# Linear attention and a routed expert layer: twelve expert tiles computed inside attention, fp32 loads on the sync queue, routing per batch

## The chip, the cores and the metric

The kernel runs on one core of one Trainium2 chip. The metric is device time in microseconds (us), the median of several executions. A profiled execution has its own span, which may differ by some us from the median. The engines are named as the profile names them: PE (matmul), PEld (weight load of PE), DVE (VectorE), ACT (ScalarE), POOL (GpSimd), SP (SyncE). The profile counts the core's 16 DMA engines together, whichever engine issues a transfer. PSUM is the memory that the matmuls write, split into tiles here named `..._ps`; a tile pool with two buffers lets one tile be filled while the other is read.

## The reference, cut to what matters

```python
def _attn_ref(q, k, v):                       # q, k, v: (8, 8, 576, 64) fp32
    q_p, k_p = phi(q), phi(k)                 # phi(x) = elu(x) + 1
    kv = np.einsum('bhsd,bhse->bhde', k_p, v)
    z = np.sum(k_p, axis=2)
    num = np.einsum('bhsd,bhde->bhse', q_p, kv)
    den = np.einsum('bhsd,bhd->bhs', q_p, z)[..., None] + 1e-06
    return num / den
# x = attention output as (4608, 512); 8 experts, F = 1024
    noisy_logits = x @ w_gate + np.log1p(np.exp(x @ w_noise)) * noise
    top2 = np.argpartition(-noisy_logits, 2, axis=1)[:, :2]   # and their softmax
    for e in range(E):
        for k in range(2):
            mask = top2[:, k] == e
            h = np.maximum(x[mask] @ w1[e], 0.0)
            out[mask] += top2_w[mask, k, None] * (h @ w2[e])
```

Each token goes to two experts: 9216 rows in all. The kernel sorts them by expert into a DRAM buffer `x_sorted` and gives every expert room for ten tiles of 128 rows, so 80 tiles. A token's second expert must add to what its first one wrote.

## The kernel before: the parts that matter

Stage 1 takes the eight batches in four groups of two: loads (cast to bf16 by GpSimd's DMA), attention, routing, then 18 scatters of 128 rows into `x_sorted`. "Ranking" is the small matmul within routing that gives each row its place. It ends a group's arithmetic, so its start time is a good mark of progress.

```python
        self.ps_kv = pool("A_ps_kv", 2, space=PSUM)     # attention: every PSUM tile twice
        self.ps_t = pool("A_ps_t", 2, space=PSUM)
        self.ps_num = pool("A_ps_num", 2, space=PSUM)
    ...
    for e in range(E):                                   # zero rows behind each expert's region
        r0 = e * REGION + 8 * P
        nc.sync.dma_start(out=x_sorted[r0 : r0 + 2 * P, :].rearrange(...), in_=...)
    with ExitStack() as actx:
        pa = PhaseA(actx, tc, q, k, v, x_sorted, c)
        pa.run()                                         # all attention, then
        for e in range(3):
            pb.load_w(e)                                 # experts
```

Stage 2 takes the experts in turn. Of each expert, transposed loads bring the rows (`xt`), PE makes `h_ps` and `y_ps`, VectorE scales `y`, and GpSimd scatters `y` into the output. From the second expert on, GpSimd first gathers what stands there (`L`), and a gather may not start before all scatters ahead of it have landed.

```python
        for e in range(E):
            ...
            for n in (512, 512, 256):
                ...                                      # load xt, h = relu(x @ w1)
                if prev is not None:
                    flush(prev)                          # y = h @ w2 of the chunk before, scatter
                if t0 == 0:
                    if e + 3 < E:
                        self.load_w(e + 3)
                    for t in range(T_CAP):               # all ten gathers of the expert in one go
                        L[t] = self.gather(gi[:, t : t + 1]) if e > 0 else None
```

## Time and profile before

The kernel before takes 584 us (median of 4 runs, 581 to 589). The profiled execution has a span of 595.4 us; its run took 597.2 us, 2.8% above the fastest. By the measure used for the other runs (slow when over 1.5% above the fastest of the same kernel) it is a slow one, so stage times of the kernel before are in sum some 13 us too long. Where these 13 us lie, no run shows.

The table of windows of the kernel before. Each row is a stretch of the span: from:to, length, then busy us of each engine with its count of instructions, the granted TensorE clock (1.00 is full), the busy share of the DMA engines, GB/s.

```profile
core 0: us, PE busy (x) PEld busy (x) DVE busy (x) ACT busy (x) POOL busy (x), PEclk, DMA share, GB/s
0.00:133.00 133.00, 44.66 (x308) 28.88 (x308) 74.86 (x242) 49.42 (x47) 69.49 (x92) 0.68 1.21 176
133.00:219.00 86.00, 36.01 (x262) 23.79 (x260) 43.23 (x149) 21.34 (x26) 36.05 (x36) 0.52 0.29 80
219.00:251.00 32.00, 0.00 (x0) 0.00 (x0) 6.68 (x38) 0.00 (x0) 17.32 (x18) 0.50 0.34 99
251.00:595.00 344.00, 292.81 (x1408) 141.84 (x1408) 97.04 (x212) 99.41 (x192) 165.84 (x170) 0.92 0.68 143
```

No engine is full before 219 us (VectorE 118 us, PE 81). Then nothing runs on PE for 32 us while the last scatters land and the first rows are loaded. Then PE is busy 293 of 344 us. The rankings, one for each group of two batches, start at 71.9, 127.4, 171.3 and 218.3 us; here they are in the view of one source line (its numbers are durations in ns, then first and last start in us):

```profile
L335 PE MATMUL kv_ps<-A,ut x4: 219/219/219, 71.9 to 218.3; 128*128 128x72 bf16 x4
```

Two groups of the page of the kernel before follow. After the bar stand busy us, mean ns of one, and the idle time of that engine just ahead of them with what ended most of it.

```profile
L483 PE MATMUL y_ps<-w,hT 128*128 128x512 bf16 x640 | 149.8, 392 | 36.5 <-DVE y L489 36.5
...
L461 POOL DMA_INDIRECT L<-out_dram,gi x70 | 70.6, 1009 | 82.1 <-DMA out_dram<-y,si 60.6
```

The gathers' idle time that is ended by a scatter landing, 60.6 us, came in 6 waits (view of waits): about one for each expert. The timeline of GpSimd shows one of them (start, us, instruction, and in brackets the idle time ahead of it):

```profile
445.05 1.08 POOL L461 DMA_INDIRECT L<-out_dram,gi  x1 [14.52 <-DMA out_dram<-y,si]
446.43 1.01 POOL L461 DMA_INDIRECT L<-out_dram,gi  x1 [0.31 <-issue]
...
456.88 1.00 POOL L461 DMA_INDIRECT L<-out_dram,gi  x1 [0.30 <-issue]
460.06 1.02 POOL L490 DMA_INDIRECT out_dram<-y,si  x1 [2.18 <-DVE gi L454]
461.38 0.99 POOL L490 DMA_INDIRECT out_dram<-y,si  x1 [0.30 <-issue]
```

### The profile page before, as it was taken

To read this page: it belongs to the slowest core of one execution; us is meant where nothing else is said; L and a number is where in the kernel's file an instruction comes from. 1 tells how busy PE (TensorE), PEld (TensorE's weight loads), DVE (VectorE), ACT (ScalarE), POOL (GpSimd) and SP (SyncE) were. 2 spreads that over 40 slices of the span, in tenths; PEclk is the share of its full clock that TensorE was granted. 3 is DMA by queue.
4 is the path that set the end of the run, shared out by engine and by line. 5 is a ranking of instruction groups with operands and counts; after the bars stand their busy time and mean duration, and the time that the engine had idled before them with its cause. 6 is when DMAs were issued, how large, how long until landed. Compare 5 with 4: busy or idle time off the path is not lost. (4 is left out here: it accounts for less than half of the span.)

```text
span 595.4 us, 5833 instructions
## 1 busy us (share of the span) xinstructions
PE 373.5 (63%) x1976; PEld 194.5 (33%) x1976; DVE 221.8 (37%) x638; ACT 170.2 (29%) x265; POOL 288.7 (48%) x315
## 2 busy tenths in 40 slices
PE   0173173137245300199989928969948968989984
PEld 0151142015124100045444404425424434444442
DVE  4359655375650560413233104314304304333122
ACT  0466444025021120062333401421511321423410
POOL 6445378427427117204346516725706726565364
PEclk9996555556555555589999978998987998998998
DMA  9999954995602002555864993993893995573153
GB/s 168 210 191 191 191 131 101 192 209 157 124 27 102 36 10 106 128 91 130 184 101 121 184 110 80 228 140 101 217 120 101 243 146 145 189 157 145 57 160 128
DMA packets 122985, 82.65 MB, mean 139 GB/s; under 512 B 74164, under 2 KB 108980, under 8 KB 122944
## 3 DMA queue, kind: packets, MB, share of 16 engines
q0 software_dynamic: 65888, 69.02, 56.8%
q1 hardware_dynamic: 54272, 12.98, 14.8%
q10 hardware_dynamic: 2784, 0.18, 0.4%
q8 instruction: 17, 0.28, 0.2%
q14 instruction: 24, 0.20, 0.1%
HBM read 80.72 MB, written 32.87 MB: 191 GB/s over the span
## 5 line engine op out<-in xcount | busy, mean ns | idle before, releaser
L474 PE MATMUL h_ps<-xt,w 128*128 128x512 bf16 (+1 forms) x768 | 150.5, 355 | 39.5 <-DMA xt<-x_sorted 32.3
L476 ACT ACTIVATE hT<-h_ps 128x512 bf16<-128x512 f32 (+1 forms) x192 | 99.4, 527 | 260.8 <-PE h_ps L474 209.2
L483 PE MATMUL y_ps<-w,hT 128*128 128x512 bf16 x640 | 149.8, 392 | 36.5 <-DVE y L489 36.5
L490 POOL DMA_INDIRECT out_dram<-y,si x80 | 79.4, 992 | 97.4 <-DVE y L487 39.9
L474 PEld LDWEIGHTS <-w 128*128 128x128 bf16 x768 | 77.8, 101 | 111.1 <-issue 46.9
L376 POOL DMA_INDIRECT x_sorted<-xrow,posi x72 | 73.6, 1022 | 78.9 <-DVE xrow L373 33.7
L461 POOL DMA_INDIRECT L<-out_dram,gi x70 | 70.6, 1009 | 82.1 <-DMA out_dram<-y,si 60.6
L483 PEld LDWEIGHTS <-hT 128*128 128x128 bf16 x640 | 64.1, 100 | 115.5 <-issue 45.3
L489 DVE SCALAR_TENSOR_TENSOR y<-y_ps,gate,L 128x512 f32<-128x512 f32 x70 | 51.1, 731 | 98.8 <-PE y_ps L483 60.6
L460 DVE MEMSET L<- 128x512 f32 x70 | 34.0, 485 | 34.4 <-DMA x_sorted<-xrow,posi 24.4
L270 PE MATMUL num_ps<-kvbd,pqt 128*128 128x162 bf16 x128 | 22.2, 324 | 38.6 <-DVE lwt L293 34.6
L203 PE MATMUL kv_ps<-v,phk 128*128 128x192 bf16 x128 | 26.0, 360 | 19.0 <-DVE phk L190 19.0
L335 PE MATMUL kv_ps<-A,ut 128*128 128x72 bf16 x4 | 0.9, 219 | 44.2 <-DVE A L331 44.2
L270 PEld LDWEIGHTS <-pqt 128*128 128x128 bf16 x128 | 13.2, 130 | 45.6 <-DVE lwt L293 41.3
L248 ACT COPY pqt<-t_ps 128x1024 bf16<-128x1024 bf16 x16 | 16.0, 1014 | 32.5 <-PE t_ps L244 10.6
L287 DVE TENSOR_TENSOR xrow<-num_ps,rden 128x512 bf16<-128x512 f32 x36 | 24.7, 687 | 0.5
L444 DVE SCALAR_TENSOR_TENSOR isf<-meta 128x10 f32<-128x10 f32 x8 | 1.4, 174 | 58.5 <-DMA meta<-x_sorted 58.5
L203 PEld LDWEIGHTS <-phk 128*128 128x128 bf16 x128 | 14.1, 131 | 23.6 <-DVE phk L190 19.0
L244 PE MATMUL t_ps<-ident,phq 128*128 128x128 bf16 x128 | 16.0, 306 | 8.0 <-ACT pqt L248 4.5
L185 ACT ACTIVATE e<-kt 128x2048 bf16<-128x2048 bf16 x8 | 15.2, 1912 | 10.7 <-DMA kt<-in_k_dram 7.9
L487 DVE TENSOR_SCALAR y<-y_ps,gate 128x512 f32<-128x512 f32 x10 | 7.5, 750 | 28.7 <-PE y_ps L483 28.7
L244 PEld LDWEIGHTS <-phq 128*128 128x128 bf16 x128 | 13.7, 144 | 9.2 <-issue 9.2
(116 smaller groups left out, 277.2 us busy)
## 6 DMA issues: line engine op xcount, KB each, us to landing
w<-in_moe_w_dram POOLq DMA_DIRECT2D x32, 512.0 KB
kt<-in_k_dram POOLq DMA_DIRECT2D x8, 512.0 KB
v<-in_v_dram POOLq DMA_DIRECT2D x8, 512.0 KB
qt<-in_q_dram POOLq DMA_DIRECT2D x8, 512.0 KB
x_sorted<-zrow SPq DMA_DIRECT2D x8, 264.0 KB, 6.6
out_dram<-y,si POOLq DMA_INDIRECT x80
x_sorted<-xrow,posi POOLq DMA_INDIRECT x72
L<-out_dram,gi POOLq DMA_INDIRECT x70
```

Source lines behind the costliest of these rows:

```text
L203: nc.tensor.matmul(out=ps[:, i, 0:192], lhsT=phk[:, hp, ci, :], rhs=vt[:, hp::4, 64 * ci : 64 * ci + 64], start=(i == 0 and ci == 0), stop ...
L244: nc.tensor.transpose(tp[:, i * 512 + ci * P : i * 512 + ci * P + P], phq[:, 2 * half + i, ci, :], c["ident"][:],)
L270: nc.tensor.matmul(out=ps[:, hp, 0:KVW], lhsT=pqs[j][:, hp, cc * P : cc * P + P], rhs=kvbds[j][:, hp, :], start=(hp % 2 == 0), stop=(hp % ...
L287: nc.vector.tensor_tensor(out=_ap(xrow[:, ci, 0:HD], [[64, 4], [256, 2], [1, 64]]), in0=_ap(ps, [[256, 4], [64, 2], [1, 64]]), in1=_ap(rd, ...
L376: r = nc.gpsimd.indirect_dma_start(out=self.x_sorted, out_offset=bass.IndirectOffsetOnAxis(ap=posi[:, ci, sl : sl + 1], axis=0), in_=xrow[ ...
L460: nc.vector.memset(L[:], 0.0)
L461: nc.gpsimd.indirect_dma_start(out=L[:].bitcast(INT32), out_offset=None, in_=self.out.bitcast(INT32), in_offset=bass.IndirectOffsetOnAxis( ...
L474: nc.tensor.matmul(out=ps[:, 0:n], lhsT=w1[:, dc, fc * P : fc * P + P], rhs=xt[:, dc, 0:n], start=(dc == 0), stop=(dc == 3))
L476: nc.scalar.activation(out=hT[:, fc, 0:n], in_=ps[:, 0:n], func=ACT.Relu)
L483: nc.tensor.matmul(out=ps[:], lhsT=hT[:, fc, t * P : t * P + P], rhs=w2[:, fc, :], start=(fc == 0), stop=(fc == 7))
L489: nc.vector.scalar_tensor_tensor(out=y[:], in0=ps[:], scalar=gate, in1=L[:], op0=ALU.mult, op1=ALU.add)
L490: r = nc.gpsimd.indirect_dma_start(out=self.out, out_offset=bass.IndirectOffsetOnAxis(ap=si, axis=0), in_=y[:], in_offset=None, bounds_che ...
```

## The change

The intent: PE has room during attention, so after four of the eight batches, with half of the tokens routed, the first 512 rows of experts 0, 1 and 2 (12 of the 80 tiles) are computed between the remaining batches. "Round two" then does the other 68 tiles. To feed this, routing is done per batch and not per pair; loads come as fp32 on the sync queue, and VectorE and ScalarE read fp32; ScalarE's queue takes the zero rows. Core of the diff:

```diff
+Q1 = 512
+E1 = 3
...
     for e in range(E):
-        r0 = e * REGION + 8 * P
-        nc.sync.dma_start(
-            out=x_sorted[r0 : r0 + 2 * P, :].rearrange("(t p) c -> p t c", p=P),
-            in_=_ap(zrow, [[0, 2], [1, ROW_W // 2]]),
-        )
+        for r0 in ([8 * P, 9 * P] if e >= E1 else [3 * P, 8 * P, 9 * P]):
+            nc.scalar.dma_start(out=x_sorted[e * REGION + r0 : e * REGION + r0 + P, :], in_=zrow[:])
...
+        ps = self.ps[b % 2] if b < NU // 2 else self.ps[0]     # two PSUM sets, then one
...
-        self.lp = pool("B_l", 12)
-        self.yp = pool("B_y", 6)
+        self.lp = pool("B_l", 4)
+        self.yp = pool("B_y", 3)
...
+        for b in range(NU // 2):
+            pa.batch(b)
+            ...
+        ld2.__exit__(None, None, None)                         # 10 of 16 load buffers
+        ps_extra.__exit__(None, None, None)                    # the second PSUM set
+        pb.open(ctx)
+        pb.psum.append(... "ps_b1", bufs=2 ...)                # ... now serve the experts
+        for b in range(NU // 2, NU):
+            ...
+            e = b - NU // 2
+            if e < E1:
+                pb.expert(e, 0, Q1 // P, col(cnt1, e), e == 0, group="read1")
+            pa.batch(b)
...
+    for e in range(3, 6):
+        pb.load_w(e, 1)
+    for e in range(E):
+        row0 = Q1 if e < E1 else 0
+        pb.expert(e, row0, T_CAP - row0 // P, col(carry, e), False)
+        if e + 6 < E:
+            pb.load_w(e + 6)
...
             hT = self.mm1(w1, xt, n)
             self.flush()
             if not first:
+                for t in range(t0, t0 + n // P):               # gathers of this chunk only: four
+                    L[t] = self.gather(gi[:, t : t + 1])
```

## The prediction

> **What bounds the kernel now.** Three stretches. (1) Attention and routing, 0 to 219 us, the last ranking matmul (timeline): no engine is full; VectorE is busy 116 of 217 us, PE 80 at a granted clock of 0.62 (table of windows). (2) A drain to 251 us: 18 scatters, 1.27 us each, then the transposed loads; PE idles 32.3 us (waits). (3) Experts, to 595 us: 80 row tiles, PE busy 293 of 345 us. At full clock a tile costs 16 matmuls of 216 ns, 3.45 us, 276 us in all; the rest is stalls, mostly GpSimd's gather waiting for the previous scatter to land (60.6 us in 6 waits), worst where a weight load shares the queue (10 to 16 us, against 2.3 without).
>
> **What the change does.**
> - 12 of 80 tiles (41 us of PE at full clock) move into the second half of attention; the last drain has 10 scatters.
> - Loads leave GpSimd's queue, with 16 fp32 buffers: attention should not starve. The nine table loads (1.28 us each) become one.
> - VectorE gets more work: eight routings instead of four (about 10 us each), casts of v, fp32 inputs. "VectorE: DVE Perf Modes" ("The perf-mode tier table") gives fp32 single-source operations 2x where bf16 gets 4x; this trace shows only bf16 (0.69 us for 2048), so I estimate 0.69 us for 1024 fp32. From traced durations I estimate 23 us per batch, 184 for eight, plus 19 for round one (8 memsets of 0.49, 12 outputs of 0.75, small ones): attention becomes VectorE-bound.
> - In the compiled order PE runs experts 0 and 1 of round one inside batch 5; they wait for batch 3's scatters (13 us) and the xt load. VectorE loses about 20 us there.
> - Round two: gathers come four at a time; each group waits until the scatters before it have landed, and the scatters for the gathers. From traced times 4 x 1.3 + 2.4 + 4 x 1.3 + 2.3 = 15.1 us per four tiles, where PE needs 13.8; about 41 us per ten-tile expert against PE's 34.5. GpSimd's chain sets the pace.
> - Weights of experts 3 to 5 (12.6 MB fp32, about 31 us at the traced rate) are issued between the last scatter and the first gather: PE stalls 10 to 20 us.
>
> **Sum (profiled scale).** Last ranking 219 -> 240 us (more VectorE work, fewer waits). From there to the end 376 -> 335 us (slow start and three six-tile experts under weight loads 127, five experts at 41, tail). 595 -> 575; unprofiled runs lie some 10 us lower: 566 us against 585.
>
> **What would show it.** VectorE busy above 80% before the last ranking, near 205 us in total there; last ranking at 225 to 260 us; PE idle 10 us or more before round one's first expert matmul; drain about 20 us; each group of gathers idle 2 to 3 us before it; ten-tile experts 38 to 43 us apart.
>
> **What would make it wrong.** Faster: routing hides in VectorE's gaps and ranking ends near 215 us, or PE's four output buffers hide GpSimd's chain. Slower: fp32 casts hold up descriptor writing ("SBUF — State Buffer", "Who interferes with whom": two-port VectorE operations block GpSimd; this trace shows scatters stretching from 0.96 to 1.48 us beside VectorE work), or round one stalls longer.
>
> Prediction 566 us, 8 in 10 between 530 and 603; faster 0.57, same 0.26, slower 0.17.

## The result and the profile after

The changed kernel takes 664.6 us (median of 4 runs, 664.2 to 667.1) against 584.4 us: slower, ratio 1.138 [1.129, 1.146]. A ratio here is the mean time of one kernel's fast runs over that of the other's of the same rounds, so it is not quite the ratio of the medians. The profiled span is 662.7 us.

The rankings of the changed kernel are now eight; these are their lines in PE's timeline:

```profile
60.51 0.19 PE L371 MATMUL kv_ps<-A,ut 128*128 128x32 bf16 x1
...
81.16 0.19 PE L371 MATMUL kv_ps<-A,ut 128*128 128x40 bf16 x1 [6.80 <-DVE A L367]
...
108.73 0.18 PE L371 MATMUL kv_ps<-A,ut 128*128 128x32 bf16 x1 [9.83 <-DVE A L367]
...
135.41 0.19 PE L371 MATMUL kv_ps<-A,ut 128*128 128x40 bf16 x1 [0.89 <-DVE A L367]
...
159.70 0.19 PE L371 MATMUL kv_ps<-A,ut 128*128 128x32 bf16 x1 [18.23 <-DVE A L367]
...
225.74 0.19 PE L371 MATMUL kv_ps<-A,ut 128*128 128x40 bf16 x1 [6.46 <-DVE A L367]
...
263.47 0.18 PE L371 MATMUL kv_ps<-A,ut 128*128 128x32 bf16 x1 [3.28 <-DVE A L367]
...
289.30 0.19 PE L371 MATMUL kv_ps<-A,ut 128*128 128x40 bf16 x1 [6.46 <-DVE A L367]
```

The first four batches are ranked at 135.4 us (before: 127.4). The other four need 154 us (before: 91). The table of windows of the changed kernel, cut at these marks:

```profile
core 0: us, PE busy (x) PEld busy (x) DVE busy (x) ACT busy (x) POOL busy (x), PEclk, DMA share, GB/s
0.00:135.00 135.00, 46.10 (x332) 29.69 (x333) 87.06 (x355) 44.52 (x60) 32.74 (x43) 1.00 0.98 251
135.00:160.00 25.00, 2.03 (x19) 1.34 (x18) 17.76 (x83) 5.71 (x10) 12.29 (x12) 1.00 0.80 232
160.00:226.00 66.00, 38.86 (x202) 18.12 (x206) 34.63 (x122) 19.98 (x31) 22.63 (x20) 0.91 0.53 135
226.00:289.00 63.00, 30.14 (x186) 16.94 (x186) 28.40 (x126) 12.55 (x22) 22.78 (x23) 0.61 0.21 65
289.00:314.00 25.00, 6.49 (x21) 2.51 (x22) 8.32 (x44) 0.00 (x0) 17.97 (x20) 0.57 0.50 135
314.00:437.00 123.00, 94.53 (x425) 44.67 (x432) 27.10 (x85) 32.98 (x64) 38.90 (x40) 0.85 0.84 153
437.00:648.00 211.00, 164.67 (x773) 79.14 (x784) 59.54 (x113) 53.54 (x104) 100.35 (x101) 0.92 0.41 117
```

VectorE is busy 168 us of the first 289, 58%, and in the second half of attention 81 of 154. It is not the bound. PE is not either (71 of 154). From 314 to 437 us the three shortened experts of round two run (18 tiles in 123 us), from 437 to 648 the five of ten tiles, 42 us each, where ten tiles at full PE speed take 34.5.

The same groups of the page, after:

```profile
L535 PE MATMUL y_ps<-w,hT 128*128 128x512 bf16 x628 | 162.9, 414 | 54.2 <-DVE y L541 49.6
...
L513 POOL DMA_INDIRECT L<-out_dram,gi x76 | 77.5, 1020 | 91.7 <-DMA out_dram<-y,si 61.2
```

The gathers now wait 61.2 us in 21 waits (view of waits) instead of 60.6 in 6, and PE waits more for VectorE's reads of `y_ps` (49.6 us, before 36.5). One period of GpSimd's timeline in a ten-tile expert:

```profile
482.67 1.04 POOL L513 DMA_INDIRECT L<-out_dram,gi  x1 [3.64 <-DMA out_dram<-y,si]
484.02 1.02 POOL L513 DMA_INDIRECT L<-out_dram,gi  x1 [0.31 <-issue]
...
486.64 1.00 POOL L513 DMA_INDIRECT L<-out_dram,gi  x1 [0.30 <-issue]
490.72 1.02 POOL L542 DMA_INDIRECT out_dram<-y,si  x1 [3.08 <-DVE L L512]
...
494.63 0.97 POOL L542 DMA_INDIRECT out_dram<-y,si  x1 [0.30 <-DVE y L541]
498.18 1.04 POOL L513 DMA_INDIRECT L<-out_dram,gi  x1 [2.58 <-DMA out_dram<-y,si]
```

Four gathers, a wait until they have landed, four scatters, a wait until they have landed: 482.67 to 498.18 is 15.5 us for four tiles.

### The profile page after: what moved, and what is told of

It reads as the page before. It is cut to its first block, busy times and chain, and to the rows that moved or that the text cites. A ratio compares the mean times of both kernels' runs of the same rounds, so it can differ in the third digit from the quotient of the medians.

```text
span 662.7 us, 6183 instructions
## 1 busy us (share of the span) xinstructions
PE 382.8 (58%) x1953; PEld 192.4 (29%) x1980; DVE 262.8 (40%) x922; ACT 169.3 (26%) x289; POOL 248.6 (38%) x257
## 5 line engine op out<-in xcount | busy, mean ns | idle before, releaser
L535 PE MATMUL y_ps<-w,hT 128*128 128x512 bf16 x628 | 162.9, 414 | 54.2 <-DVE y L541 49.6
L423 POOL DMA_INDIRECT x_sorted<-xrow,posi x72 | 75.9, 1054 | 163.0 <-DMA ld<-in_q_dram 61.9
L541 DVE SCALAR_TENSOR_TENSOR y<-y_ps,gate,L 128x512 f32<-128x512 f32 x76 | 55.2, 729 | 164.1 <-DMA L<-out_dram,gi 86.6
L513 POOL DMA_INDIRECT L<-out_dram,gi x76 | 77.5, 1020 | 91.7 <-DMA out_dram<-y,si 61.2
L535 PEld LDWEIGHTS <-hT 128*128 128x128 bf16 x640 | 66.3, 104 | 142.6 <-issue 77.8
L195 ACT ACTIVATE e<-ld 128x1024 bf16<-128x1024 f32 x32 | 33.6, 1054 | 54.4 <-DVE phk L199 12.7
L303 PE MATMUL num_ps<-kvbd,pqt 128*128 128x162 bf16 x128 | 23.2, 320 | 39.9 <-DVE lwt L326 34.5
L512 DVE MEMSET L<- 128x512 f32 x76 | 36.9, 485 | 10.4 <-DVE y L541 6.9
L243 PE MATMUL kv_ps<-v,phk 128*128 128x130 bf16 x128 | 19.2, 303 | 37.0 <-DVE phk L199 25.7
L243 PEld LDWEIGHTS <-phk 128*128 128x128 bf16 x128 | 11.9, 130 | 40.7 <-DVE phk L199 25.7
L196 DVE TENSOR_SCALAR t<-ld 128x1024 bf16<-128x1024 f32 x32 | 21.7, 685 | 2.4 <-DMA ld<-in_k_dram 2.2
```

What stands on the lines that cost most here:

```text
L195: nc.scalar.activation(out=e[:], in_=flat, func=ACT.Exp)
L243: nc.tensor.matmul(out=ps[:, i, 0:130], lhsT=phk[:, i, ci, :], rhs=vt[:, hp, ci, :], start=(i == 0 and ci == 0), stop=False, skip_group_ch ...
L303: nc.tensor.matmul(out=ps[:, hp, 0:KVW], lhsT=pqt[:, hp, ci * P : ci * P + P], rhs=kvbds[-1][:, hp, :], start=(hp % 2 == 0), stop=(hp % 2 ...
L423: r = nc.gpsimd.indirect_dma_start(out=self.x_sorted, out_offset=bass.IndirectOffsetOnAxis(ap=posi[:, ci, sl : sl + 1], axis=0), in_=xrow[ ...
L512: nc.vector.memset(L[:], 0.0)
L513: nc.gpsimd.indirect_dma_start(out=L[:].bitcast(INT32), out_offset=None, in_=self.out.bitcast(INT32), in_offset=bass.IndirectOffsetOnAxis( ...
```

## The experiments

Sixteen runs on five chips. The kernel before was run on each of them and took 583, 599, 585, 585 and 585 us (medians): one chip is 2 to 2.5% slower than the others. So I compare whole times as ratios to the kernel before on the same chip, and stages by the profiles. All results were correct, and all profiles of these runs but one (y5, below) fell in the fast state; that of the kernel before is of a slow run, as said.

| run | us | ratio to before | last ranking | from there to the end |
|---|---|---|---|---|
| before | 584 | 1 | 218.3 | 377 |
| after | 665 | 1.138 | 289.3 | 373 |
| x1_no_round1 | 667 | 1.146 | 250.0 | 413 |
| x2_gather_all | 608 | 1.045 | 289.3 | 317 |
| x3_weights_late | 676 | 1.157 | 289.0 | 384 |
| x5_zrow_pool | 641 | 1.100 | 270.6 | 366 |
| y1_no_round1_pools | 636 | 1.062 | 218.2 | 420 |
| y2_gather_zrow | 603 | 1.011 | 274.3 | 320 |
| y3_all | 579 | 0.971 | 206.1 | 367 |
| b1_before_gather4 | 654 | 1.091 | 221.4 | 433 |
| z1_no_round1_ld16 | 662 | 1.132 | 247.6 | 412 |
| z2_no_round1_psum2 | 635 | 1.086 | 215.7 | 418 |
| z3_round1_later | 663 | 1.130 | 284.0 | 378 |
| y4_weights_spread | 556 | 0.951 | 205.8 | 347 |
| b2_before_weights_mid | 565 | 0.968 | 208.7 | 355 |
| y5_round1_all_repairs | 581 | 0.992 | 264.9 | 322 |
| w1_burst_again | 557 | 0.949 | 206.0 | 350 |
| w2_spread_again | 556 | 0.948 | 207.5 | 350 |

The last two columns are from the profiled execution; the last is its span less the ranking. (y1, y2, y3 and b1 ran on the slower chip; z1 and z2 have two timed runs each, and x1, y1, z1 and z2 write 16 zero rows on ScalarE where the changed kernel writes 19.)

### 1. Take the first round away

```diff
-E1 = 3
+E1 = 0
```

(with the few lines that follow from it: expert 0 need not gather, no count is rounded up, and three of the 19 zero-row writes fall away.)

> The changed kernel with no first round (E1 = 0): per-batch routing, fp32 loads, pools and queues as in the changed kernel, all 80 tiles after the last ranking. Theory A (the first round itself costs more inside attention than its 12 tiles save later): last ranking near 240 us instead of 289, last ranking to end about 400 (373 plus 12 tiles of 3.45), whole 635 to 655 or lower, so no slower than the changed kernel's 664. Rival B (the eight routings and fp32 casts on VectorE cost the time, round one hides in gaps): last ranking stays at 275 or later, whole near 690 to 705.

Measured: 667 us, no faster and no slower than the changed kernel. Its last ranking, by the line's view, is at 250.0:

```profile
L371 PE MATMUL kv_ps<-A,ut x8: 183/188/193, 55.6 to 250.0; 128*128 128x32 bf16 x4, 128*128 128x40 bf16 x4
```

So with the 12 tiles the last ranking is 39 us later (289.3 against 250.0), and what follows is 39 us shorter (413 against 373). Of the first 39, 4 us are there at the fourth ranking already (135.4 against 131.7), before any of these tiles runs, and go with the three zero-row writes more; in the second half of attention the tiles cost 36 us (154 against 118). Neither theory had that: A was right that the first round is no gain, but it is a draw, not a loss; B was wrong, eight routings do not keep the last ranking at 275. And 250.0 is still 32 us later than in the kernel before. That and the expert stage had to be found elsewhere.

How the tiles cost this, PE's timeline of the changed kernel shows (cut; `t_ps<-ident,kvbd` are four transposes that attention of batch 5 waits for):

```profile
168.56 0.40 PE L257 MATMUL t_ps<-ident,kvbd 128*128 128x128 bf16 x2
172.91 0.58 PE L526 MATMUL h_ps<-xt,w 128*128 128x512 bf16 x1 [3.96 <-issue]
...
190.23 7.07 PE L526 MATMUL h_ps<-xt,w 128*128 128x512 bf16 x31
...
200.59 0.27 PE L257 MATMUL t_ps<-ident,kvbd 128*128 128x128 bf16 x2
```

Two of the four transposes run at 168.56. The other two stand behind the matmuls of the first round's experts 0 and 1 and run at 200.59. The Trainium skill, "TensorE: Matmul & The Clock Gate" ("Step-by-step: what each phase is for"), says that matmuls stay in program order and only weight loads are pulled ahead; this trace agrees. PE is idle for most of the second half of attention, but the idle time is not free room: it lies inside a chain of dependent steps, and a block of 28 us on PE made the step between two rankings 27 us longer (66 us against 39 without the first round).

### 2. The same twelve tiles in other places

```diff
-            e = b - NU // 2
-            if e < E1:
+            e = b - NU // 2 - 1
+            if 0 <= e < E1:
```

> The changed kernel with each expert of the first round called one batch later (before batches 5, 6, 7 instead of 4, 5, 6); in the compiled order PE then meets one expert in each of the last three batches, instead of two within batch 5. Theory K (PE's in-order queue waits for round one's inputs, whose scatters and weights are late): the step from the fifth to the sixth ranking falls from 66 to about 45 us, last ranking 265 to 275, whole 10 to 25 us faster. Rival L (the 12 tiles cost what their matmuls take, wherever they stand, because each batch is a chain that waits for them): last ranking stays within 6 us of 289, the steps only change places.

Measured: 663 us. The steps between the rankings from the fifth to the eighth, 66, 38 and 26 us in the changed kernel, are 44, 42 and 39: they change places, and the last ranking moves by 5 us only (284.0). Theory L holds: each expert of four tiles costs its matmuls wherever it stands.

### 3. What the first round took from attention

The second PSUM set and ten of the 16 load buffers go to the experts after batch 3. This run has no first round and keeps both for all eight batches:

```diff
-        ps = self.ps[b % 2] if b < NU // 2 else self.ps[0]
+        ps = self.ps[b % 2]
 ...
-        ld2.__exit__(None, None, None)          # these moved behind the last batch
-        ps_extra.__exit__(None, None, None)
```

> No first round, and both PSUM sets and all 16 load buffers kept for all eight batches (in the changed kernel the second half of attention has one PSUM set and 6 load buffers, because round one needs the room). Without the first round but with the halved room the last ranking came at 250.0 (132 us for four batches, then 118). Theory I (the halved room is most of what still separates that from the 218 of the kernel before): last ranking 225 to 238, whole 12 to 25 us below 667. Rival J (eight routings and fp32 inputs cost it): last ranking 245 or later, whole within 6 us of 667.

Measured: last ranking at 218.2, better than I expected of either theory, and where the kernel before has it (218.3; b1 below, with the same attention on the same chip as this run, has 221.4); ratio 1.062 instead of 1.146. Two runs tell the two kinds of room apart, each keeping one alone.

```diff
-        ld2.__exit__(None, None, None)          # z1: this alone moves behind the last batch
```

> No first round, 16 load buffers kept for all batches, but one PSUM set in the second half (both kept gave a last ranking at 218.2, neither at 250.0). If the load buffers are the room that matters: last ranking 218 to 226. If PSUM is: 242 to 250. A 10 us wait of VectorE for v in the fifth batch of the kernel without the room speaks for the buffers as part of it: 235 to 242 if both share it.

```diff
-        ps_extra.__exit__(None, None, None)     # z2: this alone moves, and
-        ps = self.ps[b % 2] if b < NU // 2 else self.ps[0]
+        ps = self.ps[b % 2]
```

> The counterpart: no first round, both PSUM sets kept, 6 load buffers in the second half. If PSUM is the room that matters: last ranking 218 to 228. If the load buffers are: 242 to 250.

The line's view of the run that keeps the load buffers alone, then of the run that keeps PSUM alone:

```profile
L371 PE MATMUL kv_ps<-A,ut x8: 183/188/191, 55.5 to 247.6; 128*128 128x32 bf16 x4, 128*128 128x40 bf16 x4
```

```profile
L371 PE MATMUL kv_ps<-A,ut x8: 183/189/193, 55.0 to 215.7; 128*128 128x32 bf16 x4, 128*128 128x40 bf16 x4
```

247.6 against 215.7: of the 32 us the load buffers bring 2, PSUM all of it. The Trainium skill, "PSUM — Partial Sum Buffer" ("Specifications (TRN2)"), gives eight banks of 2 KiB per partition. Attention's three tiles take 2, 2 and 4 KiB, four banks, so two sets fill PSUM, and experts can have banks only by halving attention's. These runs show the price of that: 32 us over four batches, beside the 36 us of the matmuls themselves. How it comes about is argued and not tested: with one set, PE and VectorE take turns on one `num_ps` tile. In the 55 us before the last ranking of the kernel without the first round PE waits 14.2 us there for VectorE and VectorE 12.4 us for PE; in the last 36 us of the run with both sets PE's wait is 3.4 us (views of waits).

### 4. Gathers four at a time

In the changed kernel, with more buffers as the kernel before has them:

```diff
-                for t in range(t0, t0 + n // P):
+                for t in (range(t0, t0 + n // P) if group else range(nt) if t0 == 0 else ()):
 ...
+    pb.lp = ctx.enter_context(tc.tile_pool(name="B_l2", bufs=12, side="right"))
+    pb.yp = ctx.enter_context(tc.tile_pool(name="B_y2", bufs=6, side="right"))
```

> The changed kernel, but round two issues all gathers of an expert at its first chunk, with 12 L and 6 y buffers. Theory C (gathers by fours put the scatter-gather chain of GpSimd on the path in every group): GpSimd's idle before gathers (61 us in 21 waits) falls below 40 us, the ten-tile experts come 36 to 39 us apart instead of 41.7, whole 15 to 30 us faster (634 to 650). Rival D (the chain is no longer than PE's work, the stalls come from the weight loads): whole within 8 us of 664.

Measured: 608 us, 57 us faster, twice what I expected. The ten-tile experts end 34.6 us apart, which is PE's own time. The gathers' idle time that a scatter's landing ends falls from 61.2 us in 21 waits to 18.1 in 5 (view of waits), and PE's wait for VectorE from 49.6 to 18.8 us:

```profile
L535 PE MATMUL y_ps<-w,hT 128*128 128x512 bf16 x640 | 152.1, 394 | 23.0 <-DVE y L541 18.8
...
L513 POOL DMA_INDIRECT L<-out_dram,gi x76 | 76.7, 1009 | 75.8 <-issue 31.4
```

The counter-test puts gathers by fours into the kernel before:

```diff
-                    for t in range(T_CAP):
+                for t in range(t0, t0 + n // P):
                     L[t] = self.gather(gi[:, t : t + 1]) if e > 0 else None
-        self.lp = pool("B_l", 12)
-        self.yp = pool("B_y", 6)
+        self.lp = pool("B_l", 4)
+        self.yp = pool("B_y", 3)
```

> The kernel before with its gathers issued four at a time (4 L and 3 y buffers) as the changed kernel has it, nothing else changed. Theory C (gathers by fours are the loss in the expert stage): the experts come 45 us or more apart throughout, whole 20 to 60 us slower than before (605 to 640). Rival (the loss in the changed kernel comes from its weight buffers, its x buffers or its PSUM, not from the gathers): within 8 us of 583.

Measured: 654 us, ratio 1.091; the stage after the last ranking grows from 377 to 433 us. Its experts end 53 to 57 us apart while weights are still being loaded, but only 41 to 46 us apart at the end, so "45 us or more throughout" was not met. Idle time of its gathers:

```profile
L461 POOL DMA_INDIRECT L<-out_dram,gi x70 | 71.9, 1027 | 107.5 <-DMA out_dram<-y,si 84.5
```

Both ways, the same: 0.092 and 0.091 of the kernel before's time, and 56 us by the profiles (of which those of b1 and the kernel before come from a slower chip and a slow run). Where it comes from is the round trip: the Trainium skill, "DMA: Bandwidth & Descriptors" ("Anatomy of one DMA — SWDGE (gpsimd) path"), puts the fixed cost of such a transfer at about 2.0 us, mostly waiting until the write is confirmed. The timeline above shows somewhat longer waits, 3.64, 3.08 and 2.58 us; they contain the transfer of the data too. From issue to landing the page of the changed kernel has a median of 3.3 us for gathers and 2.7 for scatters. With ten gathers in one go the trip is paid twice per expert and hidden behind PE's queued matmuls. By fours it is paid twice per four tiles, and the chain, 15.5 us, is longer than PE's 13.8. (Both runs change the numbers of `L` and `y` buffers with the grouping, since the one needs the other; they are not told apart.)

### 5. The zero rows

```diff
-            nc.scalar.dma_start(out=x_sorted[...], in_=zrow[:])
+            nc.gpsimd.dma_start(out=x_sorted[...], in_=zrow[:])
```

> The changed kernel, but the 19 zero-row writes are issued by GpSimd instead of ScalarE. Theory G (at the start ScalarE's first exponential waits 21.6 us behind its own DMA issues): first matmul at about 18 us instead of 25.7, every ranking about 7 us earlier, whole 5 to 10 us faster. Rival H (the loads or a later wait absorb it): first matmul still after 23 us, or the gain gone by the fourth ranking; whole within 3 us.

Measured: 641 us, 24 us faster, more than twice what I expected. The first lines of ScalarE's timeline in the changed kernel (ACTq is its sequencer, issuing):

```profile
10.59 12.97 ACTq L644 DMA_DIRECT2D x_sorted<-zrow  x19
23.61 0.63 ACT L228 ACTIVATE e<-km 64x512 bf16<-64x512 f32 x1 [21.58 <-DMA x_sorted<-zrow]
```

The first exponential waits 21.6 us because ScalarE's own sequencer still issues DMAs: 13 us of it for 19 zero rows. In this run it starts at 16.24 and the first ranking is 12 us earlier, the last 19 us, the end 26. The Trainium skill, "DMA: Bandwidth & Descriptors" ("Issuing engines are not separate DMA queues"), says that spreading issues over engines only saves the issuer's time, usually small beside the transfer. This agrees for one issue, 0.68 us beside 5.1 us to landing (page of the changed kernel); but 19 in a row add up, and here they stood ahead of everything. The exponential itself gains 7 us: in this run it waits for its load of k. Why the 12 us grew to 19 and 26 on the way, no run tells.

### 6. The weights

The changed kernel issues three experts' weights between the last scatters and the first gathers. Loading them one expert at a time instead, each right behind the first gathers of the expert three before it:

```diff
-    for e in range(3, 6):
-        pb.load_w(e, 1)
 ...
+            if t0 == 0 and not group and e + 3 < E:
+                with self.tc.issue_after(self.lastg):       # the chunk's last gather
+                    self.load_w(e + 3, 1)
```

> The changed kernel, but in round two weights of experts 3 to 7 are loaded one expert at a time, each behind the first gathers of the expert three before it, instead of three experts ahead of the first gathers. Theory E (the burst holds up the start of round two): the first round-two output lands near 335 us instead of 362, experts 0 to 2 take about 100 us instead of 131, whole 20 to 35 us faster. Rival F (the start is bound by the few row tiles and their latencies whoever loads): less than 8 us.

Measured: 676 us, 12 us slower. Theory E was right about the start (first output of round two at 334 us, not 362) and wrong about the sum: the stage gave it back later: experts 3 and 4 ended 57 us apart, where the changed kernel has 44. That weight loads sharing the queue with gathers and scatters did this is argued, not tested. (12 us are within the 2% by which chips differ; the profiles carry this reading.) With gathers at once and no first round, two ways of loading were written: the burst (y3, next section) and one expert at a time in the middle of an expert, away from the gathers:

```diff
             self.flush()
+            if t0 == 4 and e + 3 < E:
+                self.load_w(e + 3, 1 if e < 3 else 0)
```

> The best kernel so far (no first round, room kept, gathers at once, zero rows on GpSimd; 0.971 of before), with the weights of expert e+3 loaded in the middle of expert e instead of three experts at once ahead of the first output. If the burst slows the start of the expert stage (first expert matmul at 237.8, its second waits 8 us, GpSimd idle until 271 for the first output): first output near 258 instead of 271, whole 8 to 15 us faster, ratio 0.945 to 0.957. If later loads collide with scatters and gathers as in the kernel before, which comes 43 us apart: no gain or slower, 0.97 to 1.0.

Ratio 0.951 against 0.971 with the burst, but on another chip, and the first output did not come earlier (271 us in both), which that theory needed. So I ran both kernels again, unchanged, on one chip:

> The kernel with all four repairs and the weights of experts 3 to 5 in one burst, again, now on the same chip as its rival with the weights spread. On the slower chip its ten-tile experts came 37 to 40 us apart, where another kernel with the same gathers and the same burst had 34.6 on a faster chip. If the chip made that: 34 to 36 us apart here, and this run within 1% of the one with the weights spread. If the burst made it: 37 to 40 again, and 2% slower than the other.

> The best kernel so far, weights spread, for the pair above. If spreading is a gain of its own: ratio to before about 0.951 and 2% (10 to 14 us) below the burst. If the earlier gap was the chip's: both ratios within 1% of each other.

0.949 [0.940, 0.958] and 0.948 [0.940, 0.956]: no difference, and from the fifth expert on the experts end 34.6 us apart in both (in y3, on the slower chip, 37 to 40). The traces show why, and I had overlooked it: in the compiled program the two are the same. All 254 DMA instructions of GpSimd stand in the same order, and so do the instructions of PE, VectorE and ScalarE. The six loads for experts 3 to 5 are issued in one burst in the "spread" kernel too; its first and last (w2_spread_again):

```profile
224.91 0.81 POOL L473 DMA_DIRECT2D w<-in_moe_w_dram  x1 [2.58 <-issue]
...
228.99 0.95 POOL L474 DMA_DIRECT2D w<-in_moe_w_dram  x1
```

(in w1_burst_again at 223.48 and 227.56.) So burst against spread was not tested without a first round; y3, y4, w1 and w2 are four measurements of one program, 0.971, 0.951, 0.949 and 0.948, and the gap between the first and the others is the chip's (or its state in that session), though each was measured against the kernel before on its own chip. Where the burst really was undone, in x3, the order of issues shows it: 318, 357 and 392 us for experts 3, 4 and 5.

### 7. Repairs together, with and without the first round

The changed kernel with the edits of sections 4 and 5:

> The changed kernel with its first round, all gathers of an expert at once, and the zero rows issued by GpSimd. If the two repairs are independent the gains add: 664 - 57 - 24 = 583, within 1% of the kernel before (583). If they overlap (the zero-row gain in the expert stage, about 7 of its 24 us, came through the gather chain): 590 to 597.

The same with the edit of section 3 too (no first round, both PSUM sets and all load buffers):

> All gathers at once, zero rows on GpSimd, both PSUM sets and 16 load buffers throughout, no first round. If the first round is worth what it costs inside attention (break-even, as between the changed kernel and the one without a first round), this equals the kernel with both repairs and the first round, less what the kept room gives: 565 to 580, faster than the kernel before (583). If the first round pays once the expert stage is bound by PE: 10 to 25 us slower than that kernel.

Measured on one chip: with the first round, gathers at once and zero rows moved 603 us (1.011); without it and with both PSUM sets 579 us (0.971). Within the 2% between chips the two repairs add: they take 0.127 off the ratio, alone they took 0.092 and 0.037. And the first round, with the PSUM set it takes, costs 25 us (21 by the profiles): its last ranking is 68 us later (274.3 against 206.1), its stage after that 47 us shorter. Of the 68, about 34 would be PSUM's (section 3: 118 against 84 us for the last four batches) and 34 the tiles' own. So by this estimate the tiles alone would now gain, and the lost PSUM set is what makes the first round lose; no run has the first round with both sets.

Then the changed kernel with every repair that leaves it its first round: the edits of sections 2, 4 and 5, and the weights in the middle of an expert.

> The changed kernel with its first round and every repair that keeps it: gathers at once, zero rows on GpSimd, weights spread, first round one batch later. Against the best kernel (no first round, second PSUM set kept; 0.951): if the first round pays once PE bounds the expert stage, 0.95 or less. If its 12 tiles only change place (about 41 us later against 39 us in attention) and the PSUM set it takes costs 32 us: 20 to 30 us slower than the best kernel, 0.985 to 1.005.

And the kernel before with only its weight loads moved, and three more weight buffers:

```diff
-                if t0 == 0:
-                    if e + 3 < E:
-                        self.load_w(e + 3)
+                if t0 == 4 and e + 3 < E:
+                    self.load_w(e + 3)
+                if t0 == 0:
                     for t in range(T_CAP):
```

> The kernel before with the expert stage of the best kernel so far: six weight buffers, weights of expert e+3 loaded in the middle of expert e instead of just ahead of its gathers; attention untouched. If the best kernel's gain (ratio 0.951) is mostly the order of weight loads and owes little to the changed attention: 0.955 to 0.97 (30 us of the 42 us between the two profiled spans lie after the last ranking). If the changed attention (fp32 loads on the sync queue, routing per batch) carries it: 0.98 to 1.0.

The first: 0.992 [0.984, 1.000] (its stage times are only rough). The second: 0.968 [0.960, 0.977]. So once everything else is repaired the first round still loses 2 to 4% against the best kernel (0.948 to 0.971). And much of what the best kernel gains can be had in the kernel before by its weight loads and three more buffers, which were not told apart. There too the compiled order is not what the edit says: the weights of experts 3 to 5 are issued in a burst at 236 to 254 us, right behind the last scatters into `x_sorted`, and the last ones at 348 us (before: 476). From the fifth expert on the experts then end 34.6 us apart. Nor is attention untouched in time: its last ranking is at 208.7, since a wait of 10.2 us of ScalarE in the last group is gone; but PE's first expert matmul comes no earlier (252.5 us, before 251.1). What the changed attention adds is small against the differences between chips. By the profiles, the first expert matmul is at 237.6 us in the best kernel (y4): 3 of these 15 us are there at the last ranking (205.8 against 208.7), and behind it stand 10 scatters instead of 18, of 1.27 us each.

In the best kernel PE sets the pace from the fifth expert on: 34.6 us each, its own time. The line of the chain of waits, by engine, of the run w1_burst_again (in the kernel before it began "PE 14%; issue 4%") says less: the profile follows such a chain back over a part of the span only, 58% here and 22% there, and w2, the same program, has "PE 26%; issue 2%".

```profile
PE 46%; DMA 9%; POOL 1%; issue 1%; SPq 1%; DVE 0%; POOLq 0%; DVEq 0%
```

## Why the prediction was wrong

Predicted 566 us (530 to 603), measured 664.6. In profiled time the sum of the prediction was 240 us to the last ranking and 335 us after it; measured 289.3 and 373.4. The remaining 11 us are an offset: I took unprofiled runs to be 10 us faster than the profiled one, as with the kernel before, whose profile is of a slow run; the changed kernel's are not.

A ledger by the profiles, from 595.4 to 662.7 us:

| step | us | from |
|---|---|---|
| attention rewritten, both PSUM sets kept | 0 | 218.3 to 218.2 (before, y1) |
| second PSUM set given away | +32 | to 250.0 (x1; z1 and z2 put it on PSUM) |
| 12 tiles inside attention (36) and three more zero-row writes | +39 | to 289.3 (after) |
| the expert stage as rebuilt, all 80 tiles | +36 | 377 to 413 (before, x1) |
| 12 tiles fewer in it | -39 | 413 to 373 (after) |

By the timed runs the difference is 80 us, not 67: the 13 us by which the kernel before's profile is too slow are missing from one of the two rows that start from it, the first or the fourth. The zero rows have no row: they cost time in every kernel here that leaves them on ScalarE (on one chip the last ranking is at 218.2 with them, y1, and at 206.1 without, y3).

Point by point:

- "12 of 80 tiles (41 us of PE at full clock) move into the second half of attention": **this is the step that failed.** I counted what leaves the expert stage, and of the place it goes to I priced VectorE's work and about 20 us of waiting in batch 5; fewer waits elsewhere were to pay for part of it. So the last ranking was to move by 21 us, from 219 to 240. It moved by 71, to 289.3. The runs show that the tiles lengthen attention by 36 us, about what they save afterwards (39), and that making room for them costs 32 us more. The diff shows the PSUM set going (`ps_extra.__exit__`); I did not price it.
- "attention becomes VectorE-bound": wrong. The single cost was right: `t` from 1024 fp32 elements took 0.685 us where I estimated 0.69, half the bf16 rate, as "VectorE: DVE Perf Modes" ("The perf-mode tier table") in the Trainium skill has it. The sum was too high: VectorE's 156 us before the last ranking without the first round, where I had 184, and 168 with it, where I had about 205. And VectorE is busy 58%, not above 80%. I predicted a throughput limit for a stretch that is a chain of latencies.
- "VectorE loses about 20 us there" (batch 5): mechanism right, size low: the step from the fifth to the sixth ranking grew by 27 us beside the kernel without the first round (66 against 39), by PE's order, not for missing inputs: PE idled 4 us ahead of the first expert matmul, and not the 10 or more that I named as the sign.
- "about 41 us per ten-tile expert", gathers in chains of 15.1 us: right (42 us, 15.5 us). But I did not ask what it would be without the chains: 34.6 us, and undoing them gives 57 us.
- "slow start and three six-tile experts under weight loads 127": measured 147 us from the last ranking to the eighteenth output of round two; and a tail of 15 us where I had 3. With the five experts at 42 instead of 41 these are the 38 us by which the time after the last ranking was off. The drain took 25 us where I had about 20.
- The zero rows on ScalarE's queue: not in the prediction, and 24 us.
- Fp32 casts holding up descriptor writing, which I named as a danger: little sign; a scatter into `x_sorted` took 1.054 us on average, before 1.022 (the longest 3.39, before 1.48).

What stays open: why 12 us at the start became 26 at the end; how one PSUM set costs its 32 us; and the waits of VectorE for the scatters of `xrow` (28.1 us in 5 waits, before 4.8 in 1), which has two buffers, each for one batch now. More buffers were not run.

## What to carry to other kernels

An idle engine inside a chain of dependent steps need not be spare capacity: here work put into PE's in-order queue lengthened the chain by about its own duration, and the buffers it needed (one of two PSUM sets) cost as much again, so price the place that work moves to as well as the place it leaves. When transfers must wait for each other to land, issue all that are allowed in one go and keep enough buffers for it; and keep every early DMA issue off an engine that the first computation waits for. To compare two good versions, run them on the same chip, and look first whether their compiled order differs at all.

## What the Trainium skill lacked or had wrong

- "TensorE: Matmul & The Clock Gate" ("What's actually happening") has the clock fall to half after about 3.4 us of idle PE. That does not tell these kernels apart. Both have PE all but idle for the 32 us ahead of the first expert matmul: the kernel before (219 to 251 in its table of windows) at a granted clock of 0.50, the best kernel at 1.00, as this row of its table of windows shows (w1_burst_again). No run shows what decides it.

```profile
core 0: us, PE busy (x) PEld busy (x) DVE busy (x) ACT busy (x) POOL busy (x), PEclk, DMA share, GB/s
206.00:238.00 32.00, 0.57 (x7) 0.35 (x7) 8.52 (x44) 0.00 (x0) 14.64 (x16) 1.00 0.63 131
```

- "PSUM — Partial Sum Buffer" has the size of PSUM but no price for giving up double buffering: 32 us over four batches (250.0 against 218.2, and 215.7 with PSUM alone kept).
- "DMA: Bandwidth & Descriptors" ("Issuing engines are not separate DMA queues") calls the issue time usually small beside the DMA, which holds for one (0.68 us beside 5.1 us to landing), and does not say that issues add up on an engine that also computes. On ScalarE 19 of them took 12.97 us ahead of its first activation; moving them gave 24 us.
- No page that I read says that chips differ: the kernel before took 598.6 us on one chip (three of seven runs there were slow) and 583 to 585 on four others, and ratios taken on different chips still differed by 2% for the same kernel (0.971 and 0.949).
